# Sliding-window attention beside a gated FFN on one core: 64-row output terms of tiles three and four in one pass of the array, a v product one step earlier, and first transposes in whole squares

## The chip, the cores and the metric

The kernel runs on one core of a Trainium2 chip. A core has a matrix engine (TensorE, PE in the profile, with its weight loads listed as PEld), a vector engine (DVE), a scalar engine (ACT), GpSimd (POOL) and an engine that issues transfers (SP). Matmuls write to PSUM, eight banks of 512 float32 columns on 128 partitions; the other operands lie in SBUF. The metric is the time of one execution on the device, in microseconds (us). Times of this kernel agree within 0.1 us from run to run.

## What is computed

`x` has 2048 tokens of width D = 448. It is normalised without weights (`xn`), and the result is `x` plus causal attention with a window of 256 keys (16 heads of 28) of `xn`, plus a gated FFN of `xn` (F = 1792). All inputs are bfloat16.

```python
def _A_ref(x, wqkv, wo):
    H = 16; Dh = D // H; W = 256
    qkv = (x @ wqkv).reshape(B, S, 3, H, Dh) ...
    scores = einsum("bhqd,bhkd->bhqk", q, k) * Dh ** -0.5
    mask = (i - j >= 0) & (i - j < W)
    p = softmax(where(mask, scores, -1e9))
    o = einsum("bhqk,bhkd->bhqd", p, v)
    return o.reshape(B, S, D) @ wo

def _B_ref(x, w_gate, w_up, w_down):
    return (gelu(x @ w_gate) * (x @ w_up)) @ w_down

xn = layernorm(x)
return x + _A_ref(xn, wqkv, wo) + _B_ref(xn, w_gate, w_up, w_down)
```

## The kernel before

**Blocks.** The tokens are cut into four blocks (`qb` 0 to 3) of 512, each of four tiles of 128. Every engine's instructions stand in an order written out by hand; nothing is moved by a scheduler, but each engine waits for the semaphores of what it reads or overwrites. For each block the kernel runs the score steps of attention (`attention`, ten of them, nine in block 0), then the gate and up products of the FFN (`gated`). The down product of a block, together with its attention output times `wo`, is not run there: it is a generator, `gen_down(qb)`, that the *next* block's score steps draw on as filler for PE. The last block's runs alone at the end.

**A score step.** PE writes the scores of up to 512 columns for four heads into four PSUM banks (`sc`, one buffer), ACT takes the exponential (`p_sb`), and DVE multiplies three strips by masks at the start of the next step (`apply_masks`). The next step's scores need ACT to be done. Meanwhile PE runs what `plan[i]` lists: `(d, 12)` draws twelve matmuls from `gen_down`, `(u, 7)` draws seven steps from `gen_pairs` (v, q and k of the next block, as pairs of 64-row matmuls that write two banks) or from `gen_up`. Named items are work of other engines: `"sums"` transposes a head group's output `oc` on DVE and takes reciprocals of the sums, `"inverse"` transposes these back, and then GpSimd multiplies `oc` by them into `oN` (`scale_o`, line 593). At steps 4 and 6 `pv` runs the products of head groups 0 and 1; groups 2 and 3 (`rest`) follow the block's first gate product.

**Banks.** The four PSUM banks that the scores leave are handed out by name in turn: `take` gives the one that has been free the longest, `give` returns it in the program's order, and the next user of a bank waits for the operation that emptied it. In blocks 1 and 2 the last k pair, drawn in step 9, takes the bank of `q_last` (step 7) and the bank of the output tile that ends in step 8.

**The output sum.** A tile's output is a sum over 14 chunks of `hT` times `wd` and over four chunks of `oN` times `wo`, all 128 rows by 448 columns. The fourth chunk of `oN` has only 64 rows of content (heads 14 and 15 are folded into unused rows by a trip through DRAM, `o_collect` and `o_deliver`). For tiles 0 and 1 its two 64-row terms are issued as a pair at array rows 0 and 64 (line 409); for that, `o_finish` copies tile 1's rows to the lower half on GpSimd. For tiles 2 and 3, and for all tiles of the last block, the lower half is set to zero and the chunk is a full 128-row matmul. `end` adds `x` on DVE (line 382), and a transfer stores the tile. In the last block tile 3 is computed as two halves of 224 columns (`first`, `last`).

**The start.** The first four tiles are transposed by PE (`transp`): three squares of 128x128 and, for the last 64 dimensions, two matmuls into the two halves of the partitions (line 186), so that both halves of chunk 3 of `xnT` hold the same. The 64-row remainder of q is taken from the upper half and that of k from the lower. `v_dense(2, ...)` stands whole at the head of score step 1 in block 0.

Of the kernel before, what the change touches and what calls it, by code (L numbers as in the profile page):

```python
# [10 lines left out]
ALU = mybir.AluOpType  # L11
AX = mybir.AxisListType
bf16 = mybir.dt.bfloat16
f32 = mybir.dt.float32
# [13 lines left out]
def kernel(  # L28
# [149 lines left out]
    def transp(t, copy, tag):  # L178


        tp = psum.tile([P, 8, P], bf16, name="tp", tag=tag, bufs=1)
        xn = xns.pop(t)
        for c in range(3):
            nc.tensor.transpose(out=tp[:, c, :], in_=xn[:, c, :], identity=ident[:, :])  # L184
        for p0 in (0, 64):
            nc.tensor.transpose(out=tp[p0:p0 + 64, 3, :], in_=xn[:, 3, 0:64], identity=ident[:, :], tile_position=(0, p0))
        copy(out=xnT[:, :, t * P:(t + 1) * P], in_=tp[:, 0:4, :])

    def mm3(ps, lhs, rhs, start, stop):
        for c in range(3):  # L190
            nc.tensor.matmul(ps, lhsT=lhs(c), rhs=rhs(c), start=start and c == 0, stop=stop and c == 2,  # L191
                             skip_group_check=True)
# [25 lines left out]


    def v_dense(t, pv):  # L220
        mm3(pv, lambda c: xnT[:, c, t * P:(t + 1) * P], lambda c: wv[:, c, :], True, False)

    def v_half(t, pv):
        mm_half(pv, xnT[:, 3, t * P:(t + 1) * P], wv[:, 3, :], t % 2, False, True)
# [25 lines left out]
    def q_last(qb, copy=nc.scalar.copy):  # L250

        pq = take("pq")
        proj(pq, wqp, qb, 3)
        nc.tensor.matmul(pq, lhsT=w3p[:, 12:16, :].rearrange("p h d -> p (h d)"), rhs=xnT[:, 3, qb * QB:(qb + 1) * QB], start=False,
                         stop=True, skip_group_check=True)
        copy(out=qT[:, 3, ring(qb)], in_=pq)
        give(pq)
        done.add((qb, 3))
# [99 lines left out]
    def o_finish(qb):  # L358

        oN = oNs[qb]  # L360
        if qb < NB - 1:
            nc.gpsimd.memset(oN[64:128, 3, 2 * P:QB], 0.0)
            nc.gpsimd.tensor_copy(out=oN[64:128, 3, P:2 * P], in_=oN[0:64, 3, P:2 * P])
        else:
            nc.gpsimd.memset(oN[64:128, 3, :], 0.0)

    def gen_down(qb):

        hT, oN = hTs[qb], oNs[qb]
        fs = [(hT, wd, f) for f in range(NF)]  # L370
        main, late, os = fs[0:5] + fs[7:12], [fs[f] for f in (5, 12, 6, 13)], [(oN, wo, g) for g in range(4)]

        def begin(tt, lo=0, up=D):
            return tt, take("po", up - lo), lo, up

        def end(tt, po, lo, up):
# [5 lines left out]
            nc.vector.tensor_tensor(out=res[:, 0:w], in0=po[:, 0:w], in1=x_sb[:, t, lo:up], op=ALU.add)  # L382
            if id(po) in held:
                give(po)
            nc.sync.dma_start(out=outv[:, t, lo:up], in_=res[:, 0:w])
            last_res[:] = [res]

        def part(o, terms, start=False, stop=False):
            tt, po, lo, up = o
            w = up - lo  # L390
            for n, (x, wt, k) in enumerate(terms):
                nc.tensor.matmul(po[:, 0:w], lhsT=x[:, k, tt * P:(tt + 1) * P], rhs=wt[:, k, lo:up],  # L392
                                 start=start and n == 0, stop=stop and n == len(terms) - 1, skip_group_check=True)
                if stop and n == len(terms) - 1:
                    end(*o)
                yield

        def whole(terms, *o):
            yield from part(begin(*o), terms, True, True)

        if qb < NB - 1:
            two = [begin(tt) for tt in range(2)]
            for o in two:
                yield from part(o, main + late, True)
            for o in two:
                yield from part(o, os[0:3])
            for tt, po, *_ in two:
                r = slice(64 * tt, 64 * tt + 64)
                nc.tensor.matmul(po, lhsT=oN[r, 3, tt * P:(tt + 1) * P], rhs=wo[r, 3, :], start=False, stop=True,
                                 tile_position=(64 * tt, 0), skip_group_check=True)  # L410
            for o in two:
                end(*o)
            yield
            for tt in (2, 3):
                yield from whole(main + late + os, tt)
        else:
            two = [begin(tt) for tt in range(2)]
            for terms, start in ((main, True), (late, False)):
                for o in two:
                    yield from part(o, terms, start)  # L420
            first, last = ((3, phase[0].pool.tile([P, 2, QB], f32, name="pl", tag="s")[:, 0, 0:D // 2], lo, lo + D // 2)
                           for lo in (0, D // 2))
            yield from part(first, main + late, True)
            for o in (*two, first):
                yield from part(o, os, False, True)
            yield from part(last, main, True)
            yield from whole(main + late + os, 2)
            yield from part(last, late + os, False, True)

    def new_hT(qb):  # L430
# [300 lines left out]
    warmup(1)  # L731
    transp(1, nc.scalar.copy, "b3")
    pvs = [take("pv", D)]
    v_dense(0, pvs[0])
    norm(2)
    transp(2, nc.scalar.copy, "b2")
    norm(3)
    pads(nc.vector.tensor_copy, wqp, slice(0, 1))
    transp(3, nc.vector.tensor_copy, "b3")
    pads(nc.scalar.copy, wkp, slice(0, 1))  # L740
    swap(0)
    load_ffn(wu, B_w_up, slice(3, 5))
    nc.sync.dma_start(out=x_sb[:, 8:12, :], in_=xv[:, 8:12, :])
    pvs.append(take("pv", D))
    v_dense(1, pvs[1])
# [19 lines left out]
    v_dense(3, pvs[3])  # L765
    for dst in (wqp, wkp):
        pads(nc.vector.tensor_copy, dst, slice(2, 4))

# [32 lines left out]
    for qb in range(NB):  # L801
# [4 lines left out]
        if qb == 0:  # L806
            new_hT(0)
            early = (0, 1, 2, 3, 4)
            u = chain(gen_qk((1, 2, 3), {1: (3, pvs[3]), 2: (2, pvs[2])}), gen_up(0, (1, 2, 3, 0, 4), (3, 4)))
            w = gen_pairs(1, (("v", 0), ("v", 2), ("k", 0), ("k", 1), ("k", 2)))  # L810
            plan = [[(u, 2), ahead, (u, 1)], [lambda: v_dense(2, pvs[2]), (u, 2), ahead2, (u, 1)],
                    [lambda: spare.append(spare.pop(1)), (u, 2), ahead3, (u, 4)], [lambda: stat(8), (u, 11)],
                    [lambda: stat(9), (u, 7), lambda: stat(10), (u, 7), lambda: fill_pads(True)], ["sums", (u, 7)],
                    ["inverse", "scale", (w, 11)], [(w, 10)],
                    [lambda: stat(11), (w, 7), lambda: rstd(8, 4), "sums", "inverse", (w, 7)]]
        else:
            d = gen_down(qb - 1)
            if qb < 3:
                u = gen_pairs(qb + 1, (("v", 0), ("k", 0), ("v", 2), ("k", 1), ("k", 2)))
                plan = [[(d, 14)], [(d, 11)], [(d, 11)], [(u, 7)], [(d, 18)], ["sums", (u, 7), "inverse"], [(u, 11)],  # L820
                        [lambda: q_last(qb + 1, nc.vector.tensor_copy), (d, 6), "sums"], [(d, 2), "inverse", (d, 10)],
                        [(u, 9), "masks", (u, 1)]]
                plan[3] = [(d, 1), (u, 7)]
                if qb == 2:
                    plan[0], plan[2] = [(d, 13)], [(d, 10)]
                if qb == 1:
                    for i, j in enumerate((0, 1, 2, 4)):
                        plan[j].insert(0, lambda t=12 + i: stat(t))
                    plan[4].append(lambda: rstd(12, 4))
                    plan[1] = plan[1][:1] + [lambda: q_last(1, nc.vector.tensor_copy), (d, 8)]  # L830
                    plan[2] = plan[2][:1] + [(d, 12), lambda: collect(1)]
                    plan[4].append(lambda: deliver(1))
            else:
                new_hT(3)
                early = (1, 2, 3, 4, 5, 6)
                u = gen_up(3, early, (4, 6))
                plan = [[(u, 12)], [(u, 9)], [(d, 12)], [(d, 10)], [(d, 12)], [(d, 1), (u, 7), "sums"], [(d, 12), "inverse"],
                        ["sums", "inverse", (d, 12)], [(d, 12)], [(u, 13), "masks", (u, 1)]]
        if qb in (1, 2):
            swap(qb + 1)  # L840
        score_pool(1)
# [186 lines left out]
```

## Time and profile before

| | us |
|---|---|
| median of 3 runs (213.66 to 213.76) | 213.73 |
| the profiled execution | 213.49 |
| its span, first to last instruction | 211.7 |
| PE busy | 207.2 |
| DVE busy | 156.6 |
| ACT busy | 131.7 |
| POOL busy | 48.4 |

A row of a time line gives the start, the time taken, the engine, the line, the operation, the tile written and the tiles read, their shapes and how many instructions are merged; in brackets stands the idle time before, and what ended it. A row of the chain of work that ended last gives the start, the length, and the engine, tile and line. Group rows end with the busy time, the mean in ns of one, and the idle time before. Matmuls overlap their neighbours, so the step from one to the next is shorter than the duration of a row. Line numbers are those of the kernel before.

### The profile page before, as it was taken

The page shows a single profiled execution, that of the slowest core. Times are in us where ns is not written, and L with a number is a line of the kernel's source. Part 1 is how long each engine was busy: PE and PEld are TensorE (multiplying, and loading weights), DVE is VectorE, ACT ScalarE, POOL GpSimd, SP SyncE. Part 2 cuts the span into 40 slices and gives each one's busy share as a digit, 9 for nine tenths or more (in the row PEclk, how much of TensorE's full clock was granted, in tenths as well). Part 3 has the DMA queues.
Part 4 walks back from the last instruction along what each step waited for, and adds up shares of the span by engine and source line. Part 5 has one row for each costly group of instructions (what it writes and reads, how often), then busy time and mean ns, then how long its engine had stood idle before and what let it go on. Part 6 is the DMA issues. An engine that isn't in the chain of part 4 may idle for free.

```text
span 211.7 us, 6347 instructions
## 1 busy us (share of the span) xinstructions
PE 207.2 (98%) x2686; PEld 97.7 (46%) x2686; DVE 156.6 (74%) x355; ACT 131.7 (62%) x123; POOL 48.4 (23%) x85
## 2 busy tenths in 40 slices
PE   7999999999999999999999999999999999999994
PEld 2433444444444445444445544544444454544562
DVE  6799998999767985696437897395384699659722
ACT  4699578566777977413778787523587786757000
POOL 5287658452000220041000112013000022005100
PEclk9999999999999999999999999999999999999999
DMA  6999569978410101003421000100000011000011
GB/s 182 287 229 213 108 167 221 247 238 174 110 48 25 43 4 40 10 1 70 75 74 46 25 0 27 23 0 24 22 3 0 8 43 42 6 3 0 22 60 39
DMA packets 24889, 15.67 MB, mean 74 GB/s; under 512 B 9208, under 2 KB 24728, under 8 KB 24856
## 3 DMA queue, kind: packets, MB, share of 16 engines
q1 hardware_dynamic: 23814, 14.87, 31.1%
q8 instruction: 22, 0.36, 0.7%
q10 hardware_dynamic: 1042, 0.34, 0.7%
q14 instruction: 11, 0.09, 0.1%
HBM read 9.26 MB, written 2.41 MB: 55 GB/s over the span
## 4 chain that ended last, share of the span: by engine, by line
PE 97%; ACT 1%; issue 0%; DVE 0%; DVEq 0%; ACTq 0%
PE po L392 24%; PE gt L458 20%; PE u L458 12%; PE ue L458 8%; PE pq L334 7%; PE sc L654 7%; PE ov L626 5%; PE pv L320 4%; PE wps L150 2%; PE pq L191 2%; PE pl L392 2%; PE pv L191 1%; ACT p_sb L658 1%; PE s L191 1%; PE pk L191 1%; PE tp L184 0%
## 5 line engine op out<-in xcount | busy, mean ns | idle before, releaser
L658 ACT ACTIVATE p_sb<-sc 128x2048 bf16<-128x2048 f32 x39 | 73.2, 1878 | 20.5 <-PE sc L654 14.3
L498 ACT ACTIVATE p_sb<-gt 128x1024 bf16<-128x1024 f32 x28 | 28.7, 1025 | 33.6 <-PE gt L458 30.7
L593 POOL TENSOR_TENSOR oN<-oc,l 128x512 bf16<-128x512 f32 x16 | 21.5, 1355 | 120.2 <-DVE l L606 120.2
L458 PE MATMUL gt<-xnT,wg 64*128 64x512 bf16 x224 | 45.6, 376 | 0.0
L392 PE MATMUL po<-wd,hT 128*128 128x448 bf16 x210 | 43.3, 353 | 0.0
L458 PE MATMUL gt<-xsw,wg 64*128 64x512 bf16 x168 | 40.7, 376 | 0.0
L506 DVE TENSOR_TENSOR hT<-p_sb,u 128x512 bf16<-128x512 bf16 x34 | 21.9, 677 | 16.0 <-PE u L458 15.8
L574 DVE TENSOR_TENSOR p_sb<-p_sb,masks 128x256 bf16<-128x256 bf16 (+1 forms) x90 | 27.8, 364 | 7.6 <-ACT p_sb L658 7.6
L392 PEld LDWEIGHTS <-hT 128*128 128x128 bf16 x238 | 21.9, 98 | 19.4 <-issue 2.2
L458 PEld LDWEIGHTS <-wg 64*128 64x128 bf16 x392 | 19.0, 94 | 22.5 <-issue 0.2
L458 PEld LDWEIGHTS <-wu 64*128 64x128 bf16 x392 | 18.6, 94 | 22.5 <-issue 0.8
L458 PE MATMUL u<-xnT,wu 64*128 64x512 bf16 x136 | 28.1, 376 | 0.0
L458 PE MATMUL u<-xsw,wu 64*128 64x512 bf16 x102 | 24.7, 376 | 0.0
L458 PE MATMUL ue<-xnT,wu 64*128 64x512 bf16 x88 | 18.0, 377 | 0.0
L382 DVE TENSOR_TENSOR res<-po,x_sb 128x448 bf16<-128x448 f32 x15 | 9.0, 619 | 11.5 <-PE po L392 11.0
L654 PE MATMUL sc<-qT,kT 28*64 28x320 bf16 (+7 forms) x648 | 16.4, 261 | 0.1
L458 PE MATMUL ue<-xsw,wu 64*128 64x512 bf16 x66 | 16.4, 377 | 0.0
L584 POOL TENSOR_SCALAR_AFFINE_SELECT p_sb<-p_sb 128x512 bf16<-128x512 bf16 (+1 forms) x21 | 14.2, 703 | 6.5 <-ACT p_sb L658 6.4
L611 DVE TENSOR_TENSOR oc<-oc,ov 128x512 f32<-128x512 f32 x12 | 8.2, 681 | 8.6 <-ACT oc L610 8.6
L654 PEld LDWEIGHTS <-kT 28*64 28x64 bf16 (+1 forms) x648 | 7.5, 102 | 13.3 <-issue 12.0
L475 DVE CAST hT<-ue 128x512 bf16<-128x512 f32 x18 | 11.6, 680 | 1.9 <-PE ue L458 1.8
L392 PE MATMUL po<-wo,oN 128*128 128x448 bf16 x54 | 12.0, 352 | 0.0
(111 smaller groups left out, 280.2 us busy)
## 6 DMA issues: line engine op xcount, KB each, us to landing
out_dram<-res SPq DMA_DIRECT2D x15, 112.0 KB
wd<-in_B_w_down_dram SPq DMA_DIRECT2D x2, 784.0 KB
x_sb<-in_A_x_dram SPq DMA_DIRECT2D x3, 448.0 KB
xsw<-xnT SPq DMA_DIRECT2D x6, 192.0 KB
wu<-in_B_w_up_dram SPq DMA_DIRECT2D x4, 224.0 KB
wg<-in_B_w_gate_dram SPq DMA_DIRECT2D x2, 448.0 KB
wu<-in_B_w_up_dram SPq DMA_DIRECT2D x2, 336.0 KB
wg<-in_B_w_gate_dram SPq DMA_DIRECT2D x2, 336.0 KB
```

What stands on the lines that cost most here:

```text
L191: nc.tensor.matmul(ps, lhsT=lhs(c), rhs=rhs(c), start=start and c == 0, stop=stop and c == 2, skip_group_check=True)
L334: nc.tensor.matmul(ps, lhsT=w.rearrange("p h d -> p (h d)"), rhs=xchunk(qb, hi, c, qb * QB, QB), start=c == 0, stop=c == 6, tile_position= ...
L392: nc.tensor.matmul(po[:, 0:w], lhsT=x[:, k, tt * P:(tt + 1) * P], rhs=wt[:, k, lo:up], start=start and n == 0, stop=stop and n == len(term ...
L458: nc.tensor.matmul(ps, lhsT=w[64 * hi:64 * hi + 64, c, p * P:(p + 1) * P], rhs=xchunk(qb, hi, c, qb * QB, QB), start=c == 0, stop=c == 6, ...
L475: copy(out=hTs[qb][:, p + 7 * i, :], in_=us[i])
L498: nc.scalar.activation(out=ges[p][:, :, :], in_=gt[:, :, :], func=ACT.Gelu_apprx_tanh)
L506: nc.vector.tensor_tensor(out=hT[:, p + 7 * i, :], in0=ge[:, i, :], in1=u, op=ALU.mult)
L574: nc.vector.tensor_tensor(out=reg, in0=reg, in1=m, op=ALU.mult)
L584: nc.gpsimd.affine_select(out=reg, in_=reg, pattern=mid + [[1 if diag else -1, min(w, P)]], compare_op=ALU.is_ge, fill=0.0, base=0 if diag ...
L593: nc.gpsimd.tensor_tensor(out=oN[:, g, :], in0=oc[:, :], in1=inv, op=ALU.mult)
L654: nc.tensor.matmul(ss[k0:k0 + nk, j, col:col + nq], lhsT=kT[r, g, kt * P + k0:kt * P + k0 + nk], rhs=qT[r, g, ring(qb).start + q0:ring(qb) ...
L658: nc.scalar.activation(out=p_sb[:, :, 0:ncol], in_=ss[:, :, 0:ncol], func=ACT.Exp, scale=SCALE)
```

## The change

In `transp` the fourth square is now taken from columns 320 to 448 of `xn`, so that chunk 3 of `xnT` gets the last 64 dimensions in its lower half only; one GpSimd copy after the fourth tile fills the upper half for tokens 0 to 511. `v_dense` becomes a generator; one of tile 2's three matmuls moves from step 1 to step 0. `o_finish` copies the upper rows of tiles 1 and 3 to the lower half in one operation, for all blocks, and sets nothing to zero. In `gen_down` the fourth `oN` chunk of tiles 2 and 3 becomes a pair of 64-row matmuls. In blocks 0 and 1 the half for tile 3 goes into a bank of its own, is added to `x` in float32 (`xo`, kept in columns of `hT` that have been read) and that sum is added at the tile's end; in block 2 both tiles are finished first and the pair ends both. In the last block five halves run one after the other. The plans of blocks 1 to 3 draw one matmul less where tiles 2 and 3 end and one more item for the pair, and in blocks 1 and 2 `"sums"` and `"inverse"` of head group 0 move from step 5 to the end of step 6.

```diff
@@ transp
-        for c in range(3):
-            nc.tensor.transpose(out=tp[:, c, :], in_=xn[:, c, :], identity=ident[:, :])
-        for p0 in (0, 64):
-            nc.tensor.transpose(out=tp[p0:p0 + 64, 3, :], in_=xn[:, 3, 0:64], identity=ident[:, :], tile_position=(0, p0))
+        xf = xn[:, :, :].rearrange("p a b -> p (a b)")
+        for c, lo in enumerate((0, P, 2 * P, D - P)):
+            nc.tensor.transpose(out=tp[:, c, :], in_=xf[:, lo:lo + P], identity=ident[:, :])
@@ o_finish
-        if qb < NB - 1:
-            nc.gpsimd.memset(oN[64:128, 3, 2 * P:QB], 0.0)
-            nc.gpsimd.tensor_copy(out=oN[64:128, 3, P:2 * P], in_=oN[0:64, 3, P:2 * P])
-        else:
-            nc.gpsimd.memset(oN[64:128, 3, :], 0.0)
+        up, low = (oN[r, 3, :].rearrange("p (a b n) -> p a b n", b=2, n=P)[:, :, 1, :] for r in (slice(0, 64), slice(64, 128)))
+        nc.gpsimd.tensor_copy(out=low, in_=up)
@@ gen_down
-        main, late, os = fs[0:5] + fs[7:12], [fs[f] for f in (5, 12, 6, 13)], [(oN, wo, g) for g in range(4)]
+        main, late, os = fs[0:5] + fs[7:12], [fs[f] for f in (5, 12, 6, 13)], [(oN, wo, g) for g in range(3)]
...
+        def half(hi, o, start, stop):
+            tt, po, lo, up = o
+            r = slice(64 * hi, 64 * hi + 64)
+            nc.tensor.matmul(po[:, 0:up - lo], lhsT=oN[r, 3, tt * P:(tt + 1) * P], rhs=wo[r, 3, lo:up], start=start, stop=stop,
+                             tile_position=(64 * hi, 0), skip_group_check=True)
...
-            for tt in (2, 3):
-                yield from whole(main + late + os, tt)
+            third = begin(2)
+            yield from part(third, main + late + os, True)
+            if qb == NB - 2:
+                fourth = begin(3)
+                yield from part(fourth, main + late + os, True)
+            else:
+                fourth = begin(3)
+            half(0, third, False, True)
+            half(1, fourth, qb < NB - 2, True)
+            end(*third)
+            if qb == NB - 2:
+                end(*fourth)
+                yield
+                return
+            xo = hT[:, 0:4, 0:D // 2].bitcast(f32)
+            nc.vector.tensor_tensor(out=xo, in0=four(fourth[1]), in1=four(x_sb[:, 4 * qb + 3, :]), op=ALU.add)
+            give(fourth[1])
+            yield
+            fourth = begin(3)
+            for n, _ in enumerate(part(fourth, main + late + os, True)):
+                if n < 16:
+                    yield
+            end(*fourth, xo)
+            yield
@@ gen_down, last block
+            third = begin(2)
             for o in (*two, first):
-                yield from part(o, os, False, True)
-            yield from part(last, main, True)
-            yield from whole(main + late + os, 2)
+                yield from part(o, os)
+            for hi, o in enumerate((*two, third, first, last)):
+                half(hi % 2 if hi < 4 else 1, o, o in (third, last), o not in (third, last))
+            for o in (*two, first):
+                end(*o)
+            yield from part(last, main)
+            yield from part(third, main + late + os, False, True)
             yield from part(last, late + os, False, True)
@@ start
         transp(3, nc.vector.tensor_copy, "b3")
+        nc.gpsimd.tensor_copy(out=xnT[0:64, 3, 0:QB], in_=xnT[64:128, 3, 0:QB])
@@ plan, block 0
-            plan = [[(u, 2), ahead, (u, 1)], [lambda: v_dense(2, pvs[2]), (u, 2), ahead2, (u, 1)],
+            v2 = v_dense(2, pvs[2])
+            plan = [[(u, 2), (v2, 1), ahead, (u, 1)], [(v2, 2), (u, 2), ahead2, (u, 1)],
@@ plan, blocks 1 and 2
-                plan = [[(d, 14)], [(d, 11)], [(d, 11)], [(u, 7)], [(d, 18)], ["sums", (u, 7), "inverse"], [(u, 11)],
-                        [lambda: q_last(qb + 1, nc.vector.tensor_copy), (d, 6), "sums"], [(d, 2), "inverse", (d, 10)],
+                plan = [[(d, 14)], [(d, 11)], [(d, 11)], [(u, 7)], [(d, 17)], [(d, 1), (u, 7)], [(u, 11), "sums", "inverse"],
+                        [lambda: q_last(qb + 1, nc.vector.tensor_copy), (d, 6), "sums"], [(d, 2), "inverse", (d, 9)],
@@ plan, block 3
-                        ["sums", "inverse", (d, 12)], [(d, 12)], [(u, 13), "masks", (u, 1)]]
+                        ["sums", "inverse", (d, 11)], [(d, 11)], [(d, 1), (u, 13), "masks", (u, 1)]]
```

`end` takes the optional `rest` (here `xo`) in place of `x` as the second operand of its addition; `four` views 448 columns as 4 by 112.

More of the change, by code (lines that the diff above doesn't have):

```diff
@@ L220, in v_dense @@
     def v_dense(t, pv):
-        mm3(pv, lambda c: xnT[:, c, t * P:(t + 1) * P], lambda c: wv[:, c, :], True, False)
+        for c in range(3):
+            nc.tensor.matmul(pv, lhsT=xnT[:, c, t * P:(t + 1) * P], rhs=wv[:, c, :], start=c == 0, stop=False, skip_group_check=True)
+            yield
     def v_half(t, pv):
@@ L370, in gen_down, with four, end @@
         fs = [(hT, wd, f) for f in range(NF)]
-        main, late, os = fs[0:5] + fs[7:12], [fs[f] for f in (5, 12, 6, 13)], [(oN, wo, g) for g in range(4)]
+        main, late, os = fs[0:5] + fs[7:12], [fs[f] for f in (5, 12, 6, 13)], [(oN, wo, g) for g in range(3)]
         def begin(tt, lo=0, up=D):
             return tt, take("po", up - lo), lo, up
-        def end(tt, po, lo, up):
+        def four(a):
+            return a.rearrange("p (a b) -> p a b", a=4)
+        def end(tt, po, lo, up, rest=None):
             t, w = 4 * qb + tt, up - lo
@@ L381, in end @@
                 res = work.tile([P, D], bf16, name="res", bufs=4)
-            nc.vector.tensor_tensor(out=res[:, 0:w], in0=po[:, 0:w], in1=x_sb[:, t, lo:up], op=ALU.add)
+            if rest is None:
+                nc.vector.tensor_tensor(out=res[:, 0:w], in0=po[:, 0:w], in1=x_sb[:, t, lo:up], op=ALU.add)
+            else:
+                nc.vector.tensor_tensor(out=four(res[:, :]), in0=four(po), in1=rest, op=ALU.add)
             if id(po) in held:
@@ L396, in part @@
                 yield
-        def whole(terms, *o):
-            yield from part(begin(*o), terms, True, True)
+        def half(hi, o, start, stop):
[3 more added lines that the diff above has]
+                             tile_position=(64 * hi, 0), skip_group_check=True)
         if qb < NB - 1:
@@ L406, in gen_down @@
                 yield from part(o, os[0:3])
[L407 to L410, printed above, removed]
+            for hi, o in enumerate(two):
+                half(hi, o, False, True)
             for o in two:
@@ L413, in gen_down @@
             yield
-            for tt in (2, 3):
-                yield from whole(main + late + os, tt)
+            third = begin(2)
[3 more added lines that the diff above has]
+                yield from part(fourth, main + late + os, True)
+            else:
+                fourth = begin(3)
[15 more added lines that the diff above has]
+            end(*fourth, xo)
+            yield
         else:
@@ L733 @@
     pvs = [take("pv", D)]
-    v_dense(0, pvs[0])
+    run(v_dense(0, pvs[0]))
     norm(2)
@@ L744 @@
     pvs.append(take("pv", D))
-    v_dense(1, pvs[1])
+    run(v_dense(1, pvs[1]))
     pvs.append(take("pv", D, "b2"))
@@ L764 @@
     pvs.append(take("pv", D, "b3"))
-    v_dense(3, pvs[3])
+    run(v_dense(3, pvs[3]))
     for dst in (wqp, wkp):
```

## The prediction

> **What bounds the kernel now.** I read the page first, then the list of waits, then the chain of work that ended last, and only then the time lines of single stretches.
>
> ```profile
> PE 207.2 (98%) x2686; PEld 97.7 (46%) x2686; DVE 156.6 (74%) x355; ACT 131.7 (62%) x123; POOL 48.4 (23%) x85
> ...
> PE 97%; ACT 1%; issue 0%; DVE 0%; DVEq 0%; ACTq 0%
> ```
>
> The first row is the page's busy time by engine, the second the head of the chain. TensorE (PE) is busy for 98% of the span and holds 97% of the chain: a matmul taken out there is worth its whole step, and any wait that PE is given costs its whole length. The list of PE's waits has one row:
>
> ```profile
> PE wps L150 <- DVE wo L124: 1.4, 1, 1.4
> ```
>
> So today PE waits for no other engine after its first microsecond. The question for each edit is whether that stays so. DVE decides it: 74% over the whole span, but in the score steps of blocks 1 and 2 it runs with hardly a gap (rows below). The profiled execution took 213.49 us (span 211.7 and 1.8 around it); the median of three is 213.73, so 0.24 is added to a sum made on the profile.
>
> **The blocks: what is saved on PE.** Pieces of the chain (start, length), block 1:
>
> ```profile
> 58.39 2.38 PE po L392 x12
> ...
> 61.12 0.29 PE po L409 x2
> ...
> 63.77 3.53 PE po L392 x18
> ...
> 67.65 0.32 PE pq L334
> ```
>
> Eighteen full-array 448-column matmuls take 3.53 and twelve 2.38, so one takes (3.53 - 2.38) / 6 = 0.19, and 0.11 of each piece is the change of array shape after the scores. A pair of 64-row matmuls with that change takes 0.29, so both halves together cost 0.19: they do share the array. The change takes one full matmul from tile three and one from tile four, and adds one pair. The pair stands behind scores and ahead of 64-row matmuls, where the change of shape is paid today by the first of these (0.32 in the last row, 0.11 of it that change). Per block: -0.19 - 0.19 + 0.19 = -0.19. Step 4 loses 0.19 and step 5 gains it back; step 8 keeps the gain.
>
> **What this does to DVE in blocks 1 and 2.** The edit moves "sums" and "inverse" of head group 0 (two stream transposes and a reciprocal) from step 5 to the end of step 6, and puts two additions of a 448-column output (third tile; fourth tile's half plus x into a float32 scratch in hT) into step 5. Step 5 has room: these additions cost 0.62 each by the row at 77.83 below, stand where 1.65 of transposes went out, and the oc addition at 70.75 waits for ScalarE's copy anyway. From 70.75 on the order changes:
>
> ```profile
> 70.75 0.69 DVE L611 TENSOR_TENSOR oc<-oc,ov 128x512 f32<-128x512 f32 x1
> 71.35 1.51 DVE L574 TENSOR_TENSOR p_sb<-p_sb,masks 128x256 bf16<-128x256 bf16 x3
> 72.78 0.61 DVE L227 CAST v_sb<-pv 128x448 bf16<-128x448 f32 x1
> 73.32 0.81 DVE L574 TENSOR_TENSOR p_sb<-p_sb,masks 128x256 bf16<-128x256 bf16 x3
> 74.06 0.68 DVE L256 CAST qT<-pq 128x512 bf16<-128x512 f32 x1
> 74.66 0.70 DVE L599 STREAM_TRANSPOSE l<-oc 128x512 f32<-128x512 f32 x1
> 75.39 0.25 DVE L600 RECIPROCAL inv_all<-l 128x16 f32<-128x16 f32 x1
> 75.56 0.76 DVE L574 TENSOR_TENSOR p_sb<-p_sb,masks 128x256 bf16<-128x256 bf16 x3
> 76.23 0.70 DVE L606 STREAM_TRANSPOSE l<-inv_all 128x512 f32<-128x512 f32 x1
> 77.83 0.62 DVE L382 TENSOR_TENSOR res<-po,x_sb 128x448 bf16<-128x448 f32 x1 [0.89 <-PE po L392]
> ```
>
> ```profile
> 70.91 1.27 POOL L593 TENSOR_TENSOR oN<-oc,l 128x512 bf16<-128x512 f32 x1 [14.20 <-DVE l L606]
> ```
>
> DVE's time line and, below it, GpSimd's: start, length. Starts give the steps: oc addition 0.60, v cast 0.54, three masks 0.74 when alone (73.32 to 74.06), q cast 0.60, transpose and reciprocal 0.90. The masks at 71.35 took 1.51: GpSimd's multiply (70.91 to 72.18) held the first back until it was done. That multiply needs the "inverse". After the change group 0's inverse comes later, so it meets the masks of step 6. Block 3 already has that meeting:
>
> ```profile
> 172.04 0.70 DVE L606 STREAM_TRANSPOSE l<-inv_all 128x512 f32<-128x512 f32 x1
> 172.67 1.86 DVE L574 TENSOR_TENSOR p_sb<-p_sb,masks 128x256 bf16<-128x256 bf16 x3
> 174.46 0.70 DVE L599 STREAM_TRANSPOSE l<-oc 128x512 f32<-128x512 f32 x1
> ```
>
> ```profile
> 172.92 1.47 POOL L593 TENSOR_TENSOR oN<-oc,l 128x512 bf16<-128x512 f32 x1 [24.02 <-DVE l L606]
> ```
>
> Inverse, masks, multiply: from the masks' start to the next operation 1.79 instead of 0.74. Adding up for block 1: oc addition 70.75, masks of step 5 at 71.35 now alone to 72.09, v cast to 72.63, sums and inverse (0.73 + 0.29 with the reciprocal's hand-over + 0.63) to 74.28, masks of step 6 with the multiply (1.79) to 76.07, q cast to 76.67, sums of group 1 (0.90) to 77.57, masks of step 7 (0.67) to 78.24, inverse (0.63) to 78.87, and only then the fourth tile's output addition (0.62), done at 79.50. Today it is done at 78.45. It frees a PSUM bank, and in the changed program, as in the present one, the second bank (pk) of the last k pair is the one that this addition frees. Today that pair starts at:
>
> ```profile
> 78.74 0.38 PE L334 MATMUL pq<-xnT,wqp 64*128 64x512 bf16 x1
> ```
>
> PE now gets there 0.19 earlier, at 78.55, and goes on at 79.56: a wait of 1.0, and 0.82 later than today. Everything on PE is queued behind it: seven k steps, the first gate, the last pv products.
>
> ```profile
> 80.41 1.51 PE gt L458 x14
> 81.92 1.26 PE ov L626 x81
> ```
>
> The gate starts at 81.23, pv of group 2 ends at 83.37 and group 3 needs the bank of the last kT cast. DVE's queue up to it: masks of step 8 from 79.42 (blocked to about 80.4 by group 1's multiply, then 0.5), two casts (1.20), masks (0.74), cast (0.68): done at about 83.5, a further 0.15. Block 1: +0.97. Block 2 has the same plan:
>
> ```profile
> 120.78 0.69 DVE L611 TENSOR_TENSOR oc<-oc,ov 128x512 f32<-128x512 f32 x1
> ```
>
> ```profile
> 128.84 0.38 PE L334 MATMUL pq<-xnT,wqp 64*128 64x512 bf16 x1
> ```
>
> DVE's start lies 50.03 after block 1's, PE's need 50.10: 0.07 better, +0.90. Bounds of one block: -0.19 if the multiply never delays the masks (the addition is then done at 78.45, in time), +1.5 if it also held the transposes and casts in its way for half a microsecond.
>
> **Block 3** runs the two remaining tiles into two banks and pairs at the start of step 9: -0.19. The additions (2 x 0.62) follow the pair, and the bank is needed after 14 gate-like matmuls (1.51, as in the gate row above): hidden, between -0.19 and +0.2.
>
> **The start.** Chain and DVE rows:
>
> ```profile
> 7.44 0.17 PE tp L184 x3
> 7.61 0.18 PE tp L186 x2
> 7.79 0.27 PE tp L184 x3
> 8.06 0.18 PE tp L186 x2
> ...
> 11.87 1.89 ACT p_sb L658
> ...
> 14.20 0.68 PE pv L191 x3
> ```
>
> ```profile
> 7.16 0.40 DVE L170 TENSOR_SCALAR xn<-x_sb,mv_all,rstd_all 128x448 bf16<-128x448 bf16 x1 [0.32 <-ACT rstd_all L161]
> ```
>
> A tile's two half transposes take 0.18, a whole one 0.17 / 3 = 0.06: 0.12 saved per tile, four tiles. But tile 3's normalised input is there only at 7.56, whatever PE does, so little more than its own 0.12 remains: I take -0.15, from 0 to -0.48. The added GpSimd copy of 64x512 costs about 0.6 by its nearest row,
>
> ```profile
> L858 POOL COPY wo<-wo 64x448 bf16<-64x448 bf16 x1 | 0.6, 553 | 0.1
> ```
>
> and is needed by the half products that run after six projections, more than a microsecond later; without that cover it would cost its 0.6. The v product: step 0 ends with PE waiting for the first exponential (11.87 to 13.76), so one matmul there is free, and step 1's three (0.68) become two: -0.19. Together -0.34.
>
> **The tail.**
>
> ```profile
> 195.02 5.40 PE po L392 x28
> ...
> 201.76 1.51 PE po L392 x8
> ...
> 204.62 3.40 PE po L392 x18
> 208.02 0.78 PE pl L392 x8
> ```
>
> Three matmuls of 448 columns (0.19) and two of 224 (0.10) go out, two shared passes of 0.19 come in: -0.39. The pairs now stand inside full-array matmuls: two changes of shape, 0.11 each by the rows above, so -0.17. GpSimd's copy for the lower rows is done some 2 us ahead, since the output products start only at 201.76.
>
> The Trainium skill, "TensorEngine Tiling (Array Packing)", Key Properties, says that changing the tiling drains the array. Its page "TensorE: Matmul & The Clock Gate", Single matmul latency, puts 166 ns on a warm matmul beyond its columns; two drains at that, an estimate, would be 0.33 and leave -0.06 of the tail. The rows here show 0.11, and the sum keeps 0.11.
>
> **Sum:** -0.34 + 0.97 + 0.90 - 0.19 - 0.17 = +1.17 on 213.49, that is 214.7 in a profile and 214.9 as a median. Its own range, 214.2 to 215.6, comes from the start's and block 3's bounds and 0.3 either way on each wait.
>
> **Rivals.** (1) DVE keeps up: the masks get through ahead of the multiply, the fourth tile's addition is in time and all savings count: -0.34 - 0.57 - 0.17 = -1.08, 212.7. For it: the first mask starts before the multiply does. Against: in block 3 it did so too, and the last mask still waited. The Trainium skill, "SBUF — State Buffer", Who interferes with whom, says that the one that issues first keeps the shared port for its whole instruction and the other blocks; block 3's multiply (1.47 instead of 1.27) and mask agree, each waited in turn. (2) The delay is half as long (0.5 instead of 1.05 of blocking): a wait of 0.5, 0.3 net per block and no second wait, -0.34 + 0.6 - 0.36 = -0.1, 213.6. (3) Slower still: GpSimd's multiply holds the casts too, +1.5 a block, 216.0. It decides from the point where the q cast of step 7 starts after 76.5. (4) The halves do not share the array in the new places: 0.19 more in each of three blocks, 0.39 in the tail, 215.9; the row of 0.29 for two speaks against it.
>
> **Chances.** Forecast 0.56, (1) 0.18, (2) 0.13, (3) 0.09, (4) 0.04. About 0.2% (0.43 us) can be told from no change here. Faster is (1) and a little of (2): 0.19. Same is most of (2) and the forecast's lower edge: 0.14. Slower 0.67. To leave no more than 2 in 10 out, the range reaches into (1) and towards (3) and (4): 212.6 to 215.8.
>
> **What would show it.** Right: the list of PE's waits names the last k pair waiting for the fourth tile's addition, about 1 us, once in each of blocks 1 and 2, with that addition ending near 79.5 less the start's 0.34; the mask trio of step 6 takes about 1.8; v products start step 1 in 0.49; the tail's pairs take 0.6 with their changes of shape. Wrong: no new PE row (then (1)), the trio at 0.8, or PE waits at the start on GpSimd's copy.

## The result, and the profile after

The changed kernel takes 215.41 us (median of 6 runs, 215.17 to 215.78) against 213.75 for the kernel before in the same series: 1.0081 times as long, 95% interval 1.0067 to 1.0095. The profiled execution took 215.77 us (span 213.9). The forecast was 214.9, slower, with 212.6 to 215.8 as its range.

The page after, busy time by engine and the head of the chain of work that ended last:

```profile
PE 207.4 (97%) x2682; PEld 97.9 (46%) x2682; DVE 160.4 (75%) x357; ACT 131.6 (62%) x123; POOL 48.7 (23%) x83
...
PE 80%; DVE 12%; DMA 5%; issue 1%; ACT 1%; ACTq 0%; DVEq 0%
```

PE is busy as long as before, but 12% of the chain now runs over DVE and 5% over a transfer; before it was PE for 97%. The list of PE's waits (total, times, longest) had one row and now has five:

```profile
PE wps L150 <- DVE wo L124: 1.4, 1, 1.4
PE pk L335 <- DVE res L386: 1.1, 2, 0.6
PE pv L221 <- ACT xnT L186: 0.4, 1, 0.4
PE pk L190 <- DVE wkp L745: 0.3, 1, 0.3
PE tp L185 <- DVE xn L170: 0.2, 1, 0.2
```

The second row is the forecast's: the last k pair of blocks 1 and 2 waits for the fourth tile's output addition. Block 1 in three time lines of the changed kernel; first DVE's, with the masks of step 6, the addition, the masks of step 8 and the last kT cast:

```profile
74.57 1.86 DVE L606 TENSOR_TENSOR p_sb<-p_sb,masks 128x256 bf16<-128x256 bf16 x3
...
79.16 0.58 DVE L386 TENSOR_TENSOR res<-po,hT 128x448 bf16<-128x448 f32 x1
79.67 1.60 DVE L606 TENSOR_TENSOR p_sb<-p_sb,masks 128x256 bf16<-128x256 bf16 x3
...
83.12 0.68 DVE L246 CAST kT<-pk 128x512 bf16<-128x512 f32 x1
```

GpSimd's:

```profile
74.79 1.49 POOL L625 TENSOR_TENSOR oN<-oc,l 128x512 bf16<-128x512 f32 x1 [17.61 <-DVE l L638]
79.31 1.27 POOL L625 TENSOR_TENSOR oN<-oc,l 128x512 bf16<-128x512 f32 x1 [3.03 <-DVE l L638]
```

and PE's:

```profile
78.83 0.38 PE L335 MATMUL pq<-xnT,wqp 64*128 64x512 bf16 x1
79.79 0.37 PE L335 MATMUL pk<-xsw,wsq 64*128 64x512 bf16 x1 [0.58 <-DVE res L386]
...
82.90 1.68 PE L658 MATMUL ov<-p_sb,v_sb 64*32 64x320 bf16 x96
```

The first multiply lies inside the mask trio of step 6, the addition ends at 79.74, and the k half of the pair starts 0.05 later, 0.96 behind its q half, where before both started together (the row's 0.58 is the part in which PE was idle, after the q half's own 0.38). The last pv products take 1.68 where before they took 1.33: group 3 waits there for the bank of the last kT cast, done at 83.80.

By stages, from the first score matmul of a block to that of the next (PE's time line; the last column ends with the last matmul):

| us | first score of block 0 | of block 1 | block 1 | block 2 | block 3 and tail |
|---|---|---|---|---|---|
| before | 11.37 | 52.02 | 50.84 | 50.11 | 55.83 |
| after | 11.22 | 52.30 | 51.96 | 51.15 | 55.60 |
| difference | -0.15 | +0.28 | +1.12 | +1.04 | -0.23 |

The column of block 1's first score holds all that comes ahead of it. The four differences +0.28, +1.12, +1.04 and -0.23 make +2.2: the two profiled executions differ by 2.28, the medians by 1.66.

### The profile page after: what moved, and what is told of

It is laid out like the page before. It is cut to its first block, busy times and chain, and to the rows that moved or that the text cites. A ratio compares the mean times of both kernels' runs of the same rounds, so it can differ in the third digit from the quotient of the medians.

```text
span 213.9 us, 6335 instructions
## 1 busy us (share of the span) xinstructions
PE 207.4 (97%) x2682; PEld 97.9 (46%) x2682; DVE 160.4 (75%) x357; ACT 131.6 (62%) x123; POOL 48.7 (23%) x83
## 4 chain that ended last, share of the span: by engine, by line
PE 80%; DVE 12%; DMA 5%; issue 1%; ACT 1%; ACTq 0%; DVEq 0%
PE po L396 20%; PE gt L490 19%; PE u L490 12%; PE ue L490 8%; DVE p_sb L606 5%; PE sc L686 5%; DMA wraw<-in_A_wqkv_dram 5%; PE ov L658 4%; PE pq L335 4%; PE pv L321 3%; PE pl L396 2%; DVE l L631 1%; DVE kT L246 1%; PE pk L190 1%; PE po L405 1%; PE pq L190 1%
## 5 line engine op out<-in xcount | busy, mean ns | idle before, releaser
L625 POOL TENSOR_TENSOR oN<-oc,l 128x512 bf16<-128x512 f32 x16 | 22.2, 1394 | 120.3 <-DVE l L638 120.3
L490 PE MATMUL gt<-xsw,wg 64*128 64x512 bf16 x168 | 40.0, 376 | 0.0
L606 DVE TENSOR_TENSOR p_sb<-p_sb,masks 128x256 bf16<-128x256 bf16 (+1 forms) x90 | 30.2, 391 | 8.0 <-ACT p_sb L690 8.0
L490 PEld LDWEIGHTS <-wg 64*128 64x128 bf16 x392 | 19.8, 94 | 21.8 <-issue 0.2
L490 PEld LDWEIGHTS <-wu 64*128 64x128 bf16 x392 | 19.1, 94 | 22.3 <-issue 1.1
L384 DVE TENSOR_TENSOR res<-po,x_sb 128x448 bf16<-128x448 f32 x13 | 7.6, 619 | 8.8 <-PE po L405 5.7
L658 PE MATMUL ov<-p_sb,v_sb 64*32 64x320 bf16 (+7 forms) x648 | 11.5, 256 | 0.2
```

Of the source, the lines that this page charges most:

```text
L490: nc.tensor.matmul(ps, lhsT=w[64 * hi:64 * hi + 64, c, p * P:(p + 1) * P], rhs=xchunk(qb, hi, c, qb * QB, QB), start=c == 0, stop=c == 6, ...
L606: nc.vector.tensor_tensor(out=reg, in0=reg, in1=m, op=ALU.mult)
L625: nc.gpsimd.tensor_tensor(out=oN[:, g, :], in0=oc[:, :], in1=inv, op=ALU.mult)
L658: nc.tensor.matmul(ov[half or 0][32 * j:32 * j + 32, q0:q0 + nq], lhsT=v_sb[r, kt, 4 * g + j, :], rhs=p_sb[r, j, col:col + nq], start=n == ...
```

## Experiments

Line numbers in rows are those of the kernel that the row belongs to. Medians of the kernel before beside the experiments were 213.66, 213.74 and 213.63 in the three series.

**Sums and inverse back in step 5 (blocks 1 and 2).**

```diff
-[(d, 1), (u, 7)], [(u, 11), "sums", "inverse"],
+["sums", (d, 1), (u, 7), "inverse"], [(u, 11)],
```

> The changed kernel with sums and inverse of head group 0 put back into step 5 of blocks 1 and 2 (sums ahead of the pair, inverse behind the seven pair steps); all else as changed. Theory (VectorE's queue is late from step 6 on because this work was moved there, and meets GpSimd's multiply): both waits of a block go, so blocks 1 and 2 cost -0.19 each against before in place of +1.12 and +1.05; 215.41 - 1.31 - 1.24 = 212.9 us, and the list of PE's waits loses the row of the last k pair. Rival (the two added output additions themselves, or the pair's change of array shape, make it late): 214.6 or more, with that row still there.

Measured: 212.84 us, ratio 0.9963 (0.9949 to 0.9976), faster than both kernels. DVE's time line in block 1: masks of step 5, the fourth tile's addition, the last kT cast:

```profile
71.28 1.40 DVE L606 TENSOR_TENSOR p_sb<-p_sb,masks 128x256 bf16<-128x256 bf16 x3
...
77.56 0.62 DVE L386 TENSOR_TENSOR res<-po,hT 128x448 bf16<-128x448 f32 x1 [0.78 <-PE po L396]
...
80.78 0.68 DVE L246 CAST kT<-pk 128x512 bf16<-128x512 f32 x1
```

The addition is waiting for PE now (0.78 idle before it), not PE for the addition; the row of the k pair is gone from PE's waits. Block 1 takes 50.65 and block 2 49.93: -0.19 and -0.18 against before, the saving of the pair. All of the loss in the blocks came from where these two items (1.65 of DVE work) stand, and none from the pairs.

**The addition ahead of inverse.**

```diff
-[(d, 2), "inverse", (d, 9)]
+[(d, 11), "inverse"]
```

> The changed kernel with the fourth tile's output addition put ahead of inverse in step 8 of blocks 1 and 2. Theory (the whole VectorE queue is late, not only this one operation): the addition ends 0.6 us earlier and PE's wait of 0.58 before the last k pair goes, but the last kT cast behind it ends as late as now (near 83.8 in block 1), so that the wait only moves to the last pv products: 215.4 us, from 215.1 to 215.7. Rival (only the bank that this addition frees counts): 0.6 less in each block, 214.2.

Measured: 216.08 us, ratio 1.0122 (1.0103 to 1.0141). DVE in block 1 (addition, masks of step 8, last kT cast) and the new row among PE's waits:

```profile
78.35 0.61 DVE L386 TENSOR_TENSOR res<-po,hT 128x448 bf16<-128x448 f32 x1
...
79.51 1.86 DVE L606 TENSOR_TENSOR p_sb<-p_sb,masks 128x256 bf16<-128x256 bf16 x3
...
83.23 0.68 DVE L246 CAST kT<-pk 128x512 bf16<-128x512 f32 x1
```

```profile
PE ov L658 <- DVE kT L246: 1.5, 4, 0.6
```

The k pair no longer waits, and the wait stands at the last pv products instead, as the theory said. It fell short by 0.28 (block 1: 52.24 in place of 51.96) and 0.32 (block 2: 51.47): the later inverse sends GpSimd's second multiply fully into the masks of step 8, which take 1.86 instead of 1.60. The forecast band of 215.1 to 215.7 was missed for that reason.

**Without the first multiply.**

```diff
-            later.append((g, oc, l1[...]))
+            if g or qb not in (1, 2):
+                later.append((g, oc, l1[...]))
...
+        if qb in (1, 2):
+            nc.gpsimd.memset(oN[:, 0, :], 0.0)
```

> The changed kernel without GpSimd's multiply of head group 0 in blocks 1 and 2 (that quarter of oN is set to zero at the block's start instead, so this part of the output is missing). The moved sums and inverse stay on VectorE. Theory (a good half of the lateness is the masks of step 6 waiting for the multiply): these masks take 0.74 instead of 1.78, the addition of the fourth tile ends 1.0 earlier and PE does not wait for it; 1.0 to 1.3 less in each block, 213.0 us. Rival (the added VectorE work of 1.65 is enough by itself): masks no shorter or PE still waiting, 214.6 or more.

Measured: 213.31 us, ratio 0.9981 (0.9971 to 0.9990). DVE's time line in block 1, and GpSimd's remaining multiply:

```profile
74.53 0.79 DVE L606 TENSOR_TENSOR p_sb<-p_sb,masks 128x256 bf16<-128x256 bf16 x3
...
78.04 0.59 DVE L386 TENSOR_TENSOR res<-po,hT 128x448 bf16<-128x448 f32 x1
78.55 1.60 DVE L606 TENSOR_TENSOR p_sb<-p_sb,masks 128x256 bf16<-128x256 bf16 x3
```

```profile
78.20 1.27 POOL L627 TENSOR_TENSOR oN<-oc,l 128x512 bf16<-128x512 f32 x1 [20.63 <-DVE l L640]
```

With the multiply away the same trio takes 0.79 instead of 1.86, and blocks 1 and 2 fall to 50.88 and 50.08. So the meeting is worth a little over 1.0 on DVE and PE loses about 1.1 for it in each block. Another reading lies in the same rows: the output addition (0.59) runs beside the second multiply at its usual length, while the masks behind it do not.

**Only sums back in step 5.**

```diff
-[(d, 1), (u, 7)], [(u, 11), "sums", "inverse"],
+["sums", (d, 1), (u, 7)], [(u, 11), "inverse"],
```

> The changed kernel with only sums of head group 0 put back into step 5 of blocks 1 and 2; inverse stays at the end of step 6, so that GpSimd's multiply still meets the masks of step 6. Theory (lateness on VectorE's queue adds up: 0.9 of sums, 0.63 of inverse and some 1.0 of the masks that wait for the multiply; what PE loses is what is left beyond the slack): the mask trio stays near 1.8, the addition of the fourth tile ends 0.9 earlier and PE hardly waits for it, up to 0.2 remains at the last pv products; block 1 lasts 50.6 to 50.9 from its first score to that of block 2 (51.96 in the changed kernel, 50.84 before), 212.9 to 213.4 us. Rival (the meeting with the multiply is enough by itself): 214.5 or more.

Measured: 213.37 us, ratio 0.9979 (0.9970 to 0.9989). DVE in block 1, same three rows as above:

```profile
73.35 1.87 DVE L606 TENSOR_TENSOR p_sb<-p_sb,masks 128x256 bf16<-128x256 bf16 x3
...
77.95 0.58 DVE L386 TENSOR_TENSOR res<-po,hT 128x448 bf16<-128x448 f32 x1
...
81.91 0.68 DVE L246 CAST kT<-pk 128x512 bf16<-128x512 f32 x1
```

The trio meets the multiply in full (1.87) and PE still loses little: blocks 1 and 2 take 50.93 and 50.12, 0.28 and 0.19 more than with both items in step 5 (block 1 is 0.03 over what was expected). Neither the multiply nor the moved items alone is "the" cause: lateness on one queue adds up, and 0.9 less of it from either source takes most of PE's loss away.

**The start alone, on the kernel before.** Whole squares, GpSimd's copy and the moved v matmul, as in the diff of the change.

> The kernel before with the start's edits alone (whole squares, GpSimd's copy, one v matmul of tile 2 moved to step 0). Theory (the start's saving is real, and what the profile after showed there, a weight transfer landing 0.4 late, is chance): 213.75 - 0.34 = 213.4 us, from 213.2 to 213.6, first scores of block 1 at 51.75 when the wraw transfers are issued as early as before. Rival (the new order itself brings the transfer late or uses the time up): 213.7 to 214.1, with PE waiting for the wkp copy in most runs.

Measured: 213.47 us, ratio 0.9993 (0.9984 to 1.0003): no change that can be told. This execution reached its first score at 11.71. By step of block 0 (first score to first score):

| us | step 0 | step 1 | step 2 | step 3 |
|---|---|---|---|---|
| before | 2.43 | 2.81 | 2.70 | 3.42 |
| start alone | 2.43 | 2.62 | 2.84 | 3.54 |

Step 1 gains 0.19 and step 2 gives 0.14 back. ScalarE's time line in step 2, start alone, then before:

```profile
16.76 0.30 ACT L160 ACTIVATE lnv<-mv_all,eps_t 128x3 f32<-128x3 f32 x1 [0.30 <-DVE mv_all L156]
17.09 0.20 ACT L161 ACTIVATE rstd_all<-lnv 128x3 f32<-128x3 f32 x1
17.20 0.57 ACT L245 CAST qT<-pq 128x512 bf16<-128x512 f32 x1
17.66 1.88 ACT L659 ACTIVATE p_sb<-sc 128x2048 bf16<-128x2048 f32 x1
```

```profile
16.23 0.30 ACT L160 ACTIVATE lnv<-mv_all,eps_t 128x3 f32<-128x3 f32 x1
```

Counted from the first score, the logarithm starts at 5.05 (16.76 - 11.71) instead of 4.86 (16.23 - 11.37): 0.19 later, though PE is 0.19 earlier. It waits for statistics on DVE. Behind it come the q cast and the exponential, which ends at 19.54, and the scores of step 3 start at 19.60. DVE is late because the v matmul, now in step 0, stands ahead of that step's last projections: DVE's v cast, ahead of the statistics in its queue, waits for PE's last q projection (start alone, then before).

```profile
14.02 0.62 DVE L228 CAST v_sb<-pv 128x448 bf16<-128x448 f32 x1 [0.39 <-PE pq L196]
```

```profile
13.50 0.62 DVE L227 CAST v_sb<-pv 128x448 bf16<-128x448 f32 x1 [0.20 <-PE pq L197]
```

From the first score on it starts at 2.31 instead of 2.13. The next pair of kernels tests what this is worth.

**The first version above (sums and inverse in step 5) with the v product whole in step 1 again.**

```diff
-            plan = [[(u, 2), (v2, 1), ahead, (u, 1)], [(v2, 2), (u, 2), ahead2, (u, 1)],
+            plan = [[(u, 2), ahead, (u, 1)], [lambda: v_dense(2, pvs[2]), (u, 2), ahead2, (u, 1)],
```

> The version with sums and inverse back in step 5, and the v product of tile 2 back as a whole in step 1, as before the change. Theory (the product's 0.19 is given back in the next steps, because the exponentials and ScalarE's q cast pace them): step 1 of block 0 takes 2.81 again instead of 2.62, steps 2 and 3 together 6.12 instead of 6.26 to 6.38, and the time is that of the version with the product moved, 212.8 us within 0.2. Rival (the saving reaches the end): 213.0 or more.

Measured: 212.77 us, ratio 0.9952 (0.9937 to 0.9967), against 0.9963 (0.9949 to 0.9976) with the product moved. Steps 1 to 3 take 2.81, 2.70 and 3.42 as before the change; with it moved 2.62, 2.84 and 3.42. The move is worth 0.05 here, and no time shows it. In four of the seven other profiles with the product moved step 3 takes 3.54 and the move loses 0.07. The profiles show what decides. DVE's six normalisations in step 2 and the kT cast behind them, start alone (step 3 of 3.54) and then the first version above (3.42):

```profile
17.78 2.50 DVE L170 TENSOR_SCALAR xn<-x_sb,mv_all,rstd_all 128x448 bf16<-128x448 bf16 x6
20.20 0.68 DVE L246 CAST kT<-pk 128x512 bf16<-128x512 f32 x1
```

```profile
17.43 1.93 DVE L170 TENSOR_SCALAR xn<-x_sb,mv_all,rstd_all 128x448 bf16<-128x448 bf16 x6
19.27 0.68 DVE L246 CAST kT<-pk 128x512 bf16<-128x512 f32 x1
```

The six take 2.50 in all four profiles with 3.54 and 1.93 in all four with 3.42. In the long ones the last normalisation takes 0.73 to 0.75 instead of 0.29 and ends 0.03 to 0.04 behind a GpSimd masking operation that runs beside it. The kT cast then ends 1.28 behind step 3's first score instead of 0.71, and a `ue` matmul of step 3, due at 1.21, waits for its bank until 1.33: this is the 0.12. That GpSimd holds the normalisation up is read from the coincidence; no run tests it alone.

**The last block alone, on the kernel before.**

> The kernel before with the edit of the last block alone (five halves one after the other, GpSimd's copy of tiles 1 and 3 in the last block). Theory (0.39 taken out of PE, two changes of array shape at 0.11 put in): the stretch from the first po matmul after the last gate to the last matmul takes 0.16 less, 213.66 - 0.16 = 213.5 us. Rival (a change of shape costs more inside full-array matmuls): 213.7 or more.

Its edit is the last hunk of `gen_down` in the diff, with the two-tile copy of `o_finish` for the last block. Measured: 213.64 us, ratio 0.9995 (0.9983 to 1.0006), not to be told from no change by the time. The chain of this kernel from the tail's first matmul:

```profile
195.24 5.40 PE po L393 x28
...
203.41 0.39 PE po L402 x3
203.80 0.10 PE pl L402
203.90 1.06 PE pl L393 x10
...
208.18 0.68 PE pl L393 x7
```

From 195.24 to 208.86 are 13.62; before, 195.02 to 208.80 were 13.78: 0.16 saved. The halves take 0.49, and the ten `pl` matmuls behind them 1.06 where ten without a change of shape take 0.96 (1.34 for fourteen, before).

**Block 3 alone, on the kernel before.** Tiles three and four finished first, the pair at the head of step 9.

> The kernel before with the pair of tiles three and four in block 3 alone (both tiles finished, then the pair at the head of step 9). Theory (the pair saves 0.19, but both output additions now follow it on VectorE behind the masks of two steps, so that the second ue pair waits for a bank): from the first score of block 3 to the last matmul 0.06 less, 55.77 instead of 55.83, with a gap of 0.13 ahead of the fifteenth ue matmul of step 9. Rival (the pair's change of shape is paid twice): the same loss without a gap there.

Measured: 213.53 us in one run; block 3 and the tail take 55.76 instead of 55.83. The gap is there, and in the changed kernel as well. DVE's row of the two additions behind the pair in the changed kernel, and PE's rows around the gap, which stands ahead of the sixteenth `ue` matmul, the first to use the second bank of the second pair:

```profile
181.09 1.14 DVE L384 TENSOR_TENSOR res<-po,x_sb 128x448 bf16<-128x448 f32 x2
```

```profile
181.73 0.80 PE L490 MATMUL ue<-xnT,wu 64*128 64x512 bf16 x4
182.29 0.46 PE L490 MATMUL ue<-xsw,wu 64*128 64x512 bf16 x2
```

The additions end at 182.23 and the next `ue` matmul, which needs a bank of theirs, starts at 182.29; without the gap, two steps of 0.215 behind 181.73, it would be 182.16.

**Block 3 with sums and inverse of group 1 behind the additions.** The first version above, with

```diff
-["sums", "inverse", (d, 11)], [(d, 11)], [(d, 1), (u, 13), "masks", (u, 1)]]
+[(d, 11)], [(d, 11)], [(d, 1), "sums", "inverse", (u, 13), "masks", (u, 1)]]
```

> The version with sums and inverse of group 0 back in step 5 of blocks 1 and 2, and in block 3 sums and inverse of group 1 moved from step 7 to behind the output additions of step 9. Theory (in block 3 these two items and the masks that meet GpSimd's multiply make the additions late for the second ue pair): the additions start 0.3 to 0.5 earlier behind the pair, the gap of 0.13 ahead of the fifteenth ue matmul goes, block 3 with the tail takes 55.46 instead of 55.60, provided the ue casts behind the moved items stay off the path: 212.7 us. Rival (the casts then come too late for the last pv products): 55.6 or more, 212.8 to 213.4.

Measured: 213.29 us, ratio 0.9983 (0.9970 to 0.9995); block 3 and the tail take 55.95 instead of 55.60, the rival's figure. DVE's row of the additions and PE's of the last pv products:

```profile
178.41 1.15 DVE L384 TENSOR_TENSOR res<-po,x_sb 128x448 bf16<-128x448 f32 x2
```

```profile
183.90 0.74 PE L658 MATMUL ov<-p_sb,v_sb 64*32 64x256 bf16 x48 [0.32 <-DVE hT L507]
```

The gap in the `ue` matmuls does go, but the last pv products now wait for a `ue` cast that stands behind the moved items, with 0.32 of idle time on PE. Block 3 loses 0.35 by the exchange, so this wait costs 0.48 against the 0.13 that was removed. It is the same exchange as with the addition put first.

**The changed kernel once more.**

> The changed kernel once more, for a second profile. Theory (blocks 1 and 2 lose the same in every execution; only the start scatters, with the landing of the first transfers): block 1 takes 51.96 and block 2 51.15 again within 0.05, block 3 and the tail 55.60, and what differs lies ahead of the first score of block 1, which was at 52.30; times again between 215.1 and 215.8. Rival (the two groups of times come from the blocks): block 1 or 2 differs by 0.2 or more.

Measured: 215.34 us, ratio 1.0080 (1.0064 to 1.0095). Block 1 takes 51.95, block 2 51.15, block 3 and the tail 55.59, each within 0.01 of the first profile; the first score of block 1 is at 51.89, not 52.30. Beside the one of the first microsecond, PE's waits have only the row of the k pair left. The rest of the first profile's loss was at the start, and its chain shows what it was:

```profile
6.94 5.38 DMA wraw<-in_A_wqkv_dram
...
12.34 0.29 DVE wkp L745
```

A weight transfer landed at 12.32, and the copy of these weights, the k projection and step 0 (2.90 instead of 2.43) came late behind it. Of the nine profiles with whole squares four reached the first score by 11.22, and two of these ran into this transfer (the other is that of the version with only sums in step 5, step 0 of 2.79). In the other five DVE gets to the copy at 11.98 or later, and none waits.

## Why the prediction was right, and where it was not

**Blocks 1 and 2, +0.97 and +0.90: right, 0.15 too small each.** The order on DVE came out almost to the hundredth: with the block's own 0.28 of delay taken off, the fourth tile's addition ended at 79.46 (forecast 79.50), the pair went on at 79.51 (79.56), the last kT cast ended at 83.52 (about 83.5). The first wait was 0.05 smaller than forecast: the pair went on 0.77 later than before (79.51 against 78.74), where the sum had 0.82. The term that was too small is the second wait: the last pv products got 0.35 longer (1.68 in place of 1.33), where the sum had 0.15. The sum charged the cast's lateness against the whole of group 2's products; in the trace group 3 has to start anew behind the cast and takes its 0.73 alone.

**The meeting with GpSimd's multiply.** Its size was taken from block 3 of the profile before (1.86 there; 1.86 after), and the kernel without the multiply shows that it is the cause (0.79). By the page "SBUF — State Buffer" of the Trainium skill, Who interferes with whom, a VectorE operation with two operands in SBUF contends with a GpSimd operation that reads SBUF, and one with at most one SBUF operand, outside the modes that use both of VectorE's ports, does not. The runs agree on both: the masks are held up, the output addition with one operand in PSUM takes 0.59 beside the multiply.

**The pairs.** Blocks 1 and 2 gain 0.19 and 0.18 once nothing waits, against 0.19 forecast; the halves do share the array, which rules out rival (4). Rival (1), all savings counting, asked for DVE keeping up; this held in the version with sums and inverse in step 5, and not in the change. Rival (2), half the blocking of the masks, did not hold: the trio took its full 1.86. Its price of 0.3 a block was not tested and looks too small. With all 1.07 of the blocking taken away a block came out 1.08 and 1.07 shorter, at +0.04 and -0.03 against before, so half of it would have left about 0.5, an estimate from these figures. Rival (3) asked for the q cast of step 7 to start after 76.5; it started at 76.35, or 76.07 without the start's delay.

**Block 3, -0.19: mis-sized.** It saved 0.07. The step that failed is "The additions (2 x 0.62) follow the pair, and the bank is needed after 14 gate-like matmuls (1.51, as in the gate row above): hidden": the fourteen matmuls are shorter cover than two additions on a DVE that still has masks to finish, and 0.13 was left over.

**The tail, -0.17: right,** 0.16 measured, with five halves and the change of shape behind them at 0.59 (about 0.6 forecast). The Trainium skill, "TensorEngine Tiling (Array Packing)", Key Properties, says that a change of tiling mode drains the array. The price taken for it from the rows, 0.11 a change, held (0.10 in the last block alone). It had come from a rounded 0.19 a matmul: unrounded, the two rows of block 1 leave 0.08, and the eighteen matmuls of the tail without a change in front (3.40 against 3.53) leave 0.13. With the 166 ns that the Trainium skill, "TensorE: Matmul & The Clock Gate", Single matmul latency, gives for a single matmul beyond its columns, the tail would have gained 0.06, an estimate that the measurement does not bear out.

**The start, -0.34: wrong.** The step "step 0 ends with PE waiting for the first exponential (11.87 to 13.76), so one matmul there is free" looked at PE alone. The matmul was free at the end of step 0 (2.43 either way) and step 1 did get 0.19 shorter, but the next exponentials depend on statistics and casts behind the same step, and two steps on 0.05 is left at best, or 0.07 lost. The transposes' 0.15 can't be read from the first score alone: it came between 11.15 and 11.71 in nine profiles with whole squares (median 11.35), and at 11.37, 11.58 and 11.59 in three with halves, a spread larger than the saving. Counted from the first v product, which takes out what was late ahead of it, the first score follows after 4.66 or 4.67 in the three with halves and after 4.53 or 4.54 in seven of the nine with whole squares: 0.13 saved. In the other two (4.48 and 4.91) a transfer of `x` that landed at 9.12 and 9.30 held up DVE's statistics and the kT cast behind them (in the first of the two the first v product was late as well). An early first score also brings DVE to the weight copy before the transfer is surely there, so that some of the saving can end in that wait, as it did in the profiled execution. Why the landing scatters was not settled.

**Sum.** With the sizes measured, -0.05 for the v product, -0.13 for the transposes, +1.12, +1.04, -0.07 and -0.16 make +1.75; the medians differ by 1.66. Against the forecast's +1.17 every term came out on the slow side, by 0.01 in the tail to 0.16 at the start, so that the forecast was not saved by errors that cancel.

## What to carry to other kernels

An item that is moved to make room on a queue is late by its own length and by everything that it now meets; here 1.65 us of moved VectorE work and a collision of 1.07, in each of two blocks, turned a saving of 0.4 into a loss of 2.2. When PE waits for a bank, look how far behind the whole queue of the engine that frees it is, before you change the order of two entries: here an entry brought forward only moved the wait to the next bank, in both places where it was tried. A gap that one engine shows in one step is free only if what lies behind the inserted work on the other engines has slack in the next steps as well.

## What the runs showed of the hardware

The first score came anywhere from 11.15 to 11.71, of which the edits account for 0.13. In six of the twelve profiles the chain ahead of it runs through a transfer of `x` or of weights that landed after 5 us (`x` at 5.05 to 5.21 in three, at 9.12 and 9.30 in two, `wv` at 6.88 in one). The kernel before ranged from 213.30 to 214.57 in these series, where its first three runs lay within 0.1; runs without a profile don't show how much of that is the start. From block 1 on the stages repeat within 0.02 in every profile that has the same edits there. So differences of 0.1 to 0.2 are read from the stages of a profile; the median of the whole does not resolve them.
